# Layer 1 in slots of 12 matmuls, and the split of the next pair's operands at the end of `down`

## The chip, the cores and the metric

The kernel runs on one core of a Trainium2 chip. The metric is the device time of one execution in microseconds (us). The engines are TensorE (PE: matrix products; PEld are its weight loads), VectorE (DVE), ScalarE (ACT), GpSimd (POOL) and SyncE (SP), whose in-order queue issues all transfers between DRAM and the on-chip memory SBUF. Matrix products arrive in PSUM, a second on-chip memory.

## What is computed

Attention without a softmax, whose heads are normed by their root mean square, then a layer that takes the maximum of three projections, then a second normed layer with a gate. All data are 32-bit floats.

```python
kv = np.einsum('bhsd,bhse->bhde', k, v)            # 8 batches, 8 heads, 576 tokens, head size 64
out = np.einsum('bhsd,bhde->bhse', q, kv)
x = out / sqrt(mean(out * out, -1) + 1e-6) * g_norm   # laid out as 4608 tokens x 512
h = np.maximum(np.maximum(x @ w1, x @ w2), x @ w3)    # 512 -> 768
x = h @ w_out                                         # 768 -> 512
xn = x / sqrt(mean(x * x, -1) + 1e-6) * rms_g
g = xn @ w_gate                                       # 512 -> 1536
out = (g * sigmoid(g) * (xn @ w_val)) @ w_out2        # 1536 -> 512
```

## The kernel before

**Precision.** Every operand is held as a hi and a lo part; the product of two operands is three matmuls (hi hi, hi lo, lo hi; lines 300 to 302, and `prod3` at L611 in layer 2). To split a tile, ACT writes the hi and DVE or POOL subtracts it from the tile for the lo (`split_h`, L318 and L319, with the lo on POOL).

**Layer 1.** The 4608 tokens are nine blocks `t` of 512 (NB = 9). For a block, `do_p(t, j)` makes three projections of 12 matmuls (128x512 each) for each of six column groups j, in the PSUM tiles `p`. ACT copies the first (`s1`, L327), DVE takes the maximum with the second (`s2`, L331) and with the third (`h`, L335), and `split_h` makes `hs`. `do_o(t, j)` adds `hs` times `w_out` into four PSUM tiles `acc`, one group j later. After each projection `mid()` is called: it issues one piece of the other work.

That other work, for the block that comes next, is by token groups of 128: `ao_a` multiplies q with the head's kv (`po`, L252), takes its squares (ACT), sums them (L260), and POOL raises the mean to the power -0.5 (L264); `ao_b` scales (`xn`, L269); `do_tr` turns the result on PE (`pt`, L290) and splits it into the block's `x` (L292 on ACT, L293 on DVE). `load_q` and `load_kv` load q, k and v; `do_kv` multiplies k with v (`pk`, L233). Then there is `end1` (with `two`, `over`, `end1_rest`): at the end of a block, `acc` is copied and squared, summed over the tokens' values by PE with a matrix of ones (`pr`, L411), normed, split once more (`two`), spread by a second `pr`, and stored as `xn_d`. `pair_sums` makes the sums and differences of two stored blocks (`td`) for layer 2. Finally `store_pair`, 18 generators in the list `todo`, prepares the weights of layer 2: a raw load, a conversion of two 32-bit words to one float on ACT and DVE (L99 to L109), sums of quarters (L148 to L151), splits of the four quarters (`ws`, L159 and L160) and four stores (`wd`, L163). `pump()` steps the generators that are under way (up to `most[0]` = 2) and `pair_sums` (by `aside`); `flush()` steps the norm of `end1`.

The order of all this is that of the calls as they are written; each engine works its instructions off in this order, and waits at the first whose input isn't ready.

**Layer 2.** Block 0 is computed as it stands. The other eight blocks are taken in four pairs by a scheme of seven products in place of eight: `run_unit` makes seven products of prepared token operands (`xo`, in `XO[m, k]`) and weights (`w`, `wq`) in the PSUM tiles `ua`, `ub`, `uc`; the seventh one of a unit (`last_product`) is issued in the next. The hidden values get their own sums and differences (`t`, L486), and are split for the second product (`ho`, by `split_h`). Each part's split is put off by some `tick`s (`defer`). `down` multiplies these parts with the prepared `w_out2` (`wd`): three times for each pair, in the PSUM tiles `da`, `db` and `dc`, for two halves d of the rows: product 1 in `da` and 5 in `db` (`one`), 2 in `dc`, 6 in `da`, 3 in `db`, 7 and 4 in `da`. After each product, `slot()` ticks. `build_x` makes the operands of the next pair: three of the seven (m = 1, 2, 3) are split on the chip from the stored tokens (`xr`), hi on ACT (L545) and lo on POOL (L546), the other four are loads of `td`. It is a generator (`xs`) that is stepped in the last unit before the third `down` of a pair, and at every second slot of that `down`.

Of the kernel before, what the change touches and what calls it, by code (L numbers as in the profile page):

```python
# [34 lines left out]
def tile_kernel(ctx: ExitStack, tc, qT, k, v, gcol, w1, w2, w3, wo, wg, wv, wo2, rmsg, out):  # L35
# [67 lines left out]
    def conv_b(raw, tt):  # L103
        t, u = tt[:, 0], tt[:, 1].bitcast(I32)
        ti = t.bitcast(I32)
        nc.scalar.activation(t, t, AF.Copy, scale=2.0**-112)
# [18 lines left out]
    def store_pair(i, jp):  # L125
        if i < 2:
            srcs = [cols((wg, wv)[i], 2 * jp + k) for k in range(2)]
        else:
            srcs = [wo2[(2 * jp + k) * P:(2 * jp + k + 1) * P, :] for k in range(2)]
        raws = [load_raw(srcs[0])]  # L130
        yield
        yield
        tts = []
        for k in range(2):
            tts.append(conv_a(raws[k]))
            yield
            conv_b(raws[k], tts[k])
            if k == 0:
                raws.append(load_raw(srcs[1]))
                yield  # L140
            yield
        (t0, c0), (t1, c1) = ([tt[:, n].rearrange("p (o f) -> p o f", o=2) for n in range(2)] for tt in tts)
        if i < 2:
            quarters = [(t0[:, 0], t0[:, 1]), (t1[:, 0], t1[:, 1])]
        else:
            quarters = [(t0[:, 0], t1[:, 0]), (t0[:, 1], t1[:, 1])]
        (a11, a12), (a21, a22) = quarters
        nc.vector.tensor_tensor(c0[:, 0], a21, a22, ALU.add)  # L148
        nc.vector.tensor_tensor(c0[:, 1], c0[:, 0], a11, ALU.subtract)
        nc.vector.tensor_tensor(c1[:, 0], a11, a21, ALU.subtract)  # L150
        nc.vector.tensor_tensor(c1[:, 1], a12, c0[:, 1], ALU.subtract)  # L151
        yield
        for n, src in enumerate((quarters[0], c0, c1, quarters[1])):
            g = unit([P, 2, 2, 256], F32R, "ws")
            for o, (dst, sv) in enumerate([(g, src)] if n in (1, 2) or i < 2 else [(g[:, k], src[k]) for k in range(2)]):
                if isinstance(sv, tuple):
                    sv = (t0, t1)[n // 2]
                hi, lo = (dst[:, 0], dst[:, 1]) if len(dst.shape) == 3 else (dst[:, :, 0], dst[:, :, 1])
                nc.scalar.activation(hi, sv, AF.Copy)  # L159
                nc.vector.tensor_tensor(lo, sv, f32(hi), ALU.subtract)  # L160
            yield
            d = w_d[i, jp, n] = dp.tile([P, 2, 2, 256], F32, name="wd", tag=f"wd{i}_{jp}_{n}")
            nc.sync.dma_start(d, f32(g))  # L163
# [12 lines left out]
    def pump(n=1):  # L176
        for _ in range(n):
            aside()
            aside()
# [103 lines left out]

    def new_x(t):
# [37 lines left out]
    def do_p(t, j, mid, p=None):  # L322
# [13 lines left out]
        HT[t, j] = split_h(h, "hs")  # L336

# [54 lines left out]
    def end1(t):  # L392
        y, q = [], []
        for c in range(KC):
            y.append(yp.tile([P, TB], F32, tag="y", name="y"))
            nc.scalar.activation(y[c], acc[c], AF.Copy)
            q.append(yp.tile([P, TB], F32, tag="y", name="q"))
            nc.scalar.activation(q[c], acc[c], AF.Square)
            if c:
                nc.vector.tensor_tensor(q[0], q[0], q[c], ALU.add)  # L400
        norm.append(end1_rest(t, y, q[0], two(q[0])))

    def two(t):
        w = unit([P, 2, TB], F32R, "two")
        nc.scalar.activation(w[:, 0], t, AF.Copy)
        nc.vector.tensor_tensor(w[:, 1], t, f32(w[:, 0]), ALU.subtract)
        return w
# [7 lines left out]
    def end1_rest(t, y, q, w):  # L415
# [3 lines left out]
        q3 = q.rearrange("p (s n) -> p s n", s=NS)  # L419
# [8 lines left out]
        nc.gpsimd.tensor_tensor(rs, ms, mhalf.to_broadcast([P, NS]), ALU.pow)  # L428
        nc.vector.tensor_tensor(q3, bc(rs), id3, ALU.mult)
        w = two(q)  # L430
        yield
        pr = over(w)
        for c in range(KC):
            nc.vector.scalar_tensor_tensor(y[c], y[c], gb[:, c:c + 1], pr, ALU.mult, ALU.mult)
        yield
# [26 lines left out]
    def split_x2(i):  # L462
        t = X2.pop(i)
        x = X[NB + i // KC]
        nc.scalar.activation(x[:, 0, i % KC], t, AF.Copy)
        nc.vector.tensor_tensor(x[:, 1, i % KC], t, f32(x[:, 0, i % KC]), ALU.subtract)
# [22 lines left out]
    def pair_sums(t, y):  # L489
# [3 lines left out]
        def put(m, k, src):  # L493
            hi = tmp("th").bitcast(F32R)
            nc.scalar.activation(hi, src, AF.Copy)
            nc.vector.tensor_tensor(src.bitcast(F32R), src, f32(hi), ALU.subtract)
            return m, k, hi, src

        def store(m, k, hi, lo):
            d = t_d[n, m, k] = dp.tile([P, 2, TB], F32, name="td", tag=f"td{n}_{m}_{k}")  # L500
            nc.sync.dma_start(d[:, 0], f32(hi))
            nc.sync.dma_start(d[:, 1], lo)

        for k in range(2):
            b12, b22 = y[k], y[2 + k]
            b11, b21 = tmp("b11"), tmp("b21")
# [576 lines left out]
```

## Time and profile before

| | |
|---|---|
| median of 3 runs | 1544.07 us (1542.82 to 1544.5) |
| the profiled execution | 1542.86 us, span 1541.1 us |
| mean granted clock of PE | 0.985 of full |
| PE busy | 1486.0 us, 96% of the span |
| DVE, ACT, POOL busy | 938.5, 576.3, 460.9 us |
| moved by DMA | 313.79 MB, mean 204 GB/s |

The profile is one execution, with the start and end of every instruction. A wait is put down to the operation that ended it. The program's stages follow each other in time: first loads and first tokens until about 80 us, layer 1 with fewer tokens ready until 130 us, the rest of layer 1 until 690 us, block 0 of layer 2 until 830 us, then four pairs of some 175 us.

### The profile page before, as it was taken

To read this page: it belongs to the slowest core of one execution; us is meant where nothing else is said; L and a number is where in the kernel's file an instruction comes from. 1 tells how busy PE (TensorE), PEld (TensorE's weight loads), DVE (VectorE), ACT (ScalarE), POOL (GpSimd) and SP (SyncE) were. 2 spreads that over 40 slices of the span, in tenths; PEclk is the share of its full clock that TensorE was granted. 3 is DMA by queue.
4 is the path that set the end of the run, shared out by engine and by line. 5 is a ranking of instruction groups with operands and counts; after the bars stand their busy time and mean duration, and the time that the engine had idled before them with its cause. 6 is when DMAs were issued, how large, how long until landed. Compare 5 with 4: busy or idle time off the path is not lost.

```text
span 1541.1 us, 19959 instructions
## 1 busy us (share of the span) xinstructions
PE 1486.0 (96%) x7200; PEld 1226.3 (80%) x7200; DVE 938.5 (61%) x1418; ACT 576.3 (37%) x1027; POOL 460.9 (30%) x360
## 2 busy tenths in 40 slices
PE   5899999998999989999999999999999999999998
PEld 5787888786787878878888888788887888778887
DVE  4875556676657675773333656754756746755756
ACT  3443333434344434341322432433433432434432
POOL 2444222221312121211231422523425323433323
PEclk8999999999999999999999999999999999999999
DMA  9322247258445733564686854586546845576442
GB/s 318 119 69 93 73 158 254 95 207 305 171 143 206 264 124 116 215 244 191 241 316 219 316 199 177 219 315 244 195 186 251 322 186 211 219 281 238 166 176 102
DMA packets 132513, 313.79 MB, mean 204 GB/s; under 512 B 12352, under 2 KB 43072, under 8 KB 132416
## 3 DMA queue, kind: packets, MB, share of 16 engines
q1 hardware_dynamic: 132416, 312.53, 56.1%
q8 instruction: 57, 0.93, 0.2%
q14 instruction: 40, 0.33, 0.1%
HBM read 239.08 MB, written 73.40 MB: 203 GB/s over the span
## 4 chain that ended last, share of the span: by engine, by line
PE 50%; POOL 3%; issue 2%; ACT 1%; DVE 0%; POOLq 0%; DVEq 0%
PE ua L611 15%; PE ub L611 8%; PE da L611 8%; PE uc L611 4%; PE db L611 4%; POOL ho L319 2%; PE dc L611 2%; PE acc L301 1%; PE acc L300 1%; PE acc L302 1%; PE pv L302 1%; PE p L302 1%; PE pg L302 1%; PE pv L300 1%; PE pg L300 1%
## 5 line engine op out<-in xcount | busy, mean ns | idle before, releaser
L300 PE MATMUL p<-x,w 128*128 128x512 f32 (+1 forms) x652 | 263.1, 404 | 14.5 <-DVE h L335 9.8
L301 PE MATMUL p<-x,w 128*128 128x512 f32 (+1 forms) x652 | 258.4, 396 | 0.3 <-DVE x L293 0.3
L302 PE MATMUL p<-x,w 128*128 128x512 f32 (+1 forms) x652 | 258.3, 396 | 0.0
L611 PE MATMUL ua<-xo,w 128*128 128x512 f32 x864 | 213.4, 389 | 0.0
L319 POOL TENSOR_TENSOR ho<-sl,ho 128x512 fp32r<-128x512 f32 x72 | 99.2, 1385 | 319.9 <-issue 185.1
L611 PEld LDWEIGHTS ua<-xo,w 128*128 128x128 f32 x864 | 162.2, 188 | 33.6
L319 POOL TENSOR_TENSOR hs<-h,hs 128x512 fp32r<-128x512 f32 x54 | 69.6, 1288 | 394.9 <-ACT hs L318 371.8
L319 POOL TENSOR_TENSOR ho<-t,ho 128x512 fp32r<-128x512 f32 x96 | 125.5, 1311 | 117.9 <-ACT ho L318 110.6
L300 PEld LDWEIGHTS p<-x,w 128*128 128x128 f32 x652 | 126.4, 194 | 42.8 <-DVE h L335 11.3
L302 PEld LDWEIGHTS p<-x,w 128*128 128x128 f32 x652 | 126.0, 193 | 26.6
L301 PEld LDWEIGHTS p<-x,w 128*128 128x128 f32 x652 | 126.4, 194 | 25.9 <-DVE x L293 1.0
L611 PE MATMUL ub<-xo,w 128*128 128x512 f32 x576 | 146.1, 389 | 0.0
L611 PEld LDWEIGHTS ub<-xo,w 128*128 128x128 f32 x576 | 108.1, 188 | 22.4
L693 ACT ACTIVATE s<-ua 128x512 f32<-128x512 f32 x96 | 57.2, 596 | 151.4 <-PE ua L611 136.8
L318 ACT ACTIVATE hs<-h 128x512 fp32r<-128x512 f32 x54 | 34.1, 632 | 195.7 <-DVE h L335 183.3
L611 PE MATMUL da<-ho,wd 128*128 128x512 f32 x432 | 105.8, 389 | 0.0
L318 ACT ACTIVATE ho<-t 128x512 fp32r<-128x512 f32 x96 | 59.3, 627 | 103.3 <-DVE t L486 100.6
L611 PEld LDWEIGHTS da<-ho,wd 128*128 128x128 f32 x432 | 81.1, 188 | 16.9
L264 POOL TENSOR_TENSOR rs<-ms,mhalf 128x8 f32<-128x8 f32 x36 | 61.7, 1720 | 107.8 <-DVE ms L262 102.1
L300 PE MATMUL acc<-hs,w 128*128 128x512 f32 x216 | 84.9, 393 | 0.0
L641 DVE TENSOR_TENSOR c<-uc,s 128x512 f32<-128x512 f32 x48 | 33.1, 689 | 84.7 <-PE uc L611 84.7
L301 PE MATMUL acc<-hs,w 128*128 128x512 f32 x216 | 84.2, 390 | 0.5 <-POOL hs L319 0.5
(135 smaller groups left out, 2689.0 us busy)
## 6 DMA issues: line engine op xcount, KB each, us to landing
w<-wd SPq DMA_DIRECT2D x180, 512.0 KB, 7.7
wd<-ws SPq DMA_DIRECT2D x72, 512.0 KB, 3.7
wd<-wd SPq DMA_DIRECT2D x72, 512.0 KB, 6.9
wq<-wd SPq DMA_DIRECT2D x72, 256.0 KB, 7.9
xo<-td SPq DMA_DIRECT2D x32, 512.0 KB, 7.3
raw<-in_w SPq DMA_DIRECT2D x18, 512.0 KB, 8.2
q<-in_qT SPq DMA_DIRECT2D x18, 512.0 KB, 6.0
raw<-in_wo SPq DMA_DIRECT2D x18, 512.0 KB, 6.3
```

Source lines behind the costliest of these rows:

```text
L264: nc.gpsimd.tensor_tensor(rs, ms, mhalf.to_broadcast([P, H]), ALU.pow)
L300: nc.tensor.matmul(o, ah, bh, start=first, stop=False)
L301: nc.tensor.matmul(o, ah, bl, start=False, stop=False)
L302: nc.tensor.matmul(o, al, bh, start=False, stop=last)
L318: nc.scalar.activation(hs[:, 0], h, AF.Copy)
L319: nc.gpsimd.tensor_tensor(hs[:, 1], h, f32(hs[:, 0]), ALU.subtract)
L611: nc.tensor.matmul(o, aa, bb, start=first and q == 0, stop=last and q == 2, skip_group_check=True)
L641: nc.vector.tensor_tensor(t, p, s, ALU.add)
L693: nc.scalar.activation(t, p, AF.Copy)
```

## The change

**Layer 1.** A slot is 12 matmuls. `do_p` calls `mid` after each of its projections (a new argument `last` is called after the third), and `slot()` is called once more after `do_o`: four slots for each j, 24 for a block. `slot()` calls `tick`, `flush`, `aside` and `prep`. `tick` now also fires a table, `plan`: `at(n, fn)` sets `fn` for the n-th slot from now. A group of 128 tokens is five steps in five slots (`token`): products, scales, `ao_b`, turned, low. q is loaded at slots 0 and 5 of a block, its readers are the tokens at slots 1, 5, 9 and 13; k and v are loaded four slots ahead of `do_kv`. `end1` becomes a generator of ten steps, one a slot, where `flush` was called some slots apart. `pair_sums` has one step a slot, with its tiles in the pools `raw` and `y`. `store_pair` becomes the class `Prep` with 14 steps, of which at most two are live, and which can start only while there is room for its buffers; in it, the lo of each odd quarter is made on POOL and no longer on DVE, and a store comes a slot after its lo.

**Layer 2.** In block 0 the same `slot` is called. In `down` the two groups of product 6 come before the two of product 2. `build_x` issues its loads first, and then the three splits, each lo a step after its hi; it is not stepped in `run_unit` any more, but in `down` from slot 3 on, without slots 7, 9 and 11.

```diff
+            for g in range(2):
+                self.steps.append((0, lambda g=g: (self.put(i, jp, g), self.lo(g + 1), self.hi(g + 2))))
...
+        def lo(self, n):
+            for hi, lo, src in self.halves(n):
+                (nc.gpsimd if n % 2 else nc.vector).tensor_tensor(lo, src, f32(hi), ALU.subtract)
...
+    def token(n, i):
+
+        for m, fn in enumerate(token_steps(i)):
+            at(n + m, fn)
...
-    def do_p(t, j, mid, p=None):
+    def do_p(t, j, mid, p=None, last=None):
...
         HT[t, j] = split_h(h, "hs")
+        if last is not None:
+            last()
...
-        for m, r in ((1, 0), (5, None), (2, 1), (6, None), (3, 2), (7, None), (4, None)):
+        for m in (5, 6, 7, 4):
             for k in range(2):
-                x = unit([P, 2, TB], F32R, "xo")
-                if r is None:
-                    nc.sync.dma_start(f32(x), t_d[n, m, k])
-                else:
-                    nc.scalar.activation(x[:, 0], raw[:, r, k], AF.Copy)
-                    nc.gpsimd.tensor_tensor(x[:, 1], raw[:, r, k], f32(x[:, 0]), ALU.subtract)
-                XO[m, k] = x
+                x = XO[m, k] = unit([P, 2, TB], F32R, "xo")
+                nc.sync.dma_start(f32(x), t_d[n, m, k])
             yield
+        for m, r in ((1, 0), (2, 1), (3, 2)):
+            for k in range(2):
+                x = XO[m, k] = unit([P, 2, TB], F32R, "xo")
+                nc.scalar.activation(x[:, 0], raw[:, r, k], AF.Copy)
+            yield
+            for k in range(2):
+                x = XO[m, k]
+                nc.gpsimd.tensor_tensor(x[:, 1], raw[:, r, k], f32(x[:, 0]), ALU.subtract)
...
+        for fn in plan.pop(n_slot[0], ()):
+            fn()
+        n_slot[0] += 1
+
+    def at(n, fn):
+        plan.setdefault(n_slot[0] + n, []).append(fn)
+
+    def slot():
+        tick()
+        flush()
+        aside()
+        prep()
...
-            if xs is not None and n_x[0] % 2 == 0:
+            if xs is not None and n_x[0] > 2 and n_x[0] not in (7, 9, 11):
                 next(xs, 0)
...
         one(1)
         for d in range(2):
+            prod_down(d, ph, 6, acc[d][0])
+            keep(d, 1, acc[d][0])
+            slot()
+        for d in range(2):
             c = psum([P, TB], "dc")
             prod_down(d, ph, 2, c, True)
             put(d, 0, c)
             slot()
-        for d in range(2):
-            prod_down(d, ph, 6, acc[d][0])
-            keep(d, 1, acc[d][0])
-            slot()
...
+                at(0, lambda i=base // 2: load_q(i))
+                at(5, lambda i=base // 2 + 1: load_q(i))
+                at(3, lambda t=t: new_x(t + 1))
+                for n in range(NS):
+                    token(4 * n + 1, base + n)
...
-                do_p(t, j, pump)
-                if 1 <= j <= 4:
-                    flush()
+                do_p(t, j, slot, None, slot)
```

How the instructions stand on the engines, at three places. A row is a line of the program, an operation, the tile that it writes and those that it reads, and the size; x12 is a run of twelve.

PE in the third `down` of the first pair, before:

```order
L611 MATMUL da<-ho,wd 128x512 x6
L611 MATMUL db<-ho,wd 128x512 x6
L611 MATMUL dc<-ho,wd 128x512 x12
L611 MATMUL da<-ho,wd 128x512 x12
L611 MATMUL db<-ho,wd 128x512 x12
```

The same place in the changed kernel:

```order
L760 MATMUL da<-ho,wd 128x512 x6
L760 MATMUL db<-ho,wd 128x512 x6
L760 MATMUL da<-ho,wd 128x512 x12
L760 MATMUL dc<-ho,wd 128x512 x12
L760 MATMUL db<-ho,wd 128x512 x12
```

The twelve matmuls of product 6 in `da` now stand ahead of those in `dc`. POOL at the same place, before:

```order
L546 TENSOR_TENSOR xo<-xr,xo 128x512 x2
L319 TENSOR_TENSOR ho<-t_8383,ho 128x512
L319 TENSOR_TENSOR ho<-sl,ho 128x512
L319 TENSOR_TENSOR ho<-t_8490,ho 128x512
L319 TENSOR_TENSOR ho<-t_8514,ho 128x512
L546 TENSOR_TENSOR xo<-xr,xo 128x512 x2
L319 TENSOR_TENSOR ho<-sl,ho 128x512 x2
L319 TENSOR_TENSOR ho<-t_8516,ho 128x512
L546 TENSOR_TENSOR xo<-xr,xo 128x512 x2
```

And in the changed kernel:

```order
L421 TENSOR_TENSOR ho<-sl,ho 128x512
L421 TENSOR_TENSOR ho<-t_8464,ho 128x512
L421 TENSOR_TENSOR ho<-t_8488,ho 128x512
L421 TENSOR_TENSOR ho<-sl,ho 128x512 x2
L421 TENSOR_TENSOR ho<-t_8490,ho 128x512
L421 TENSOR_TENSOR ho<-t_8522,ho 128x512
L683 TENSOR_TENSOR xo<-xr,xo 128x512 x6
```

The six `xo` stood in three pairs between the hidden parts, and stand behind them all in one row. DVE in layer 1, in the j of block 4 that follows its first, before (L107 to L109 and L99 are the weight conversion):

```order
L107 TENSOR_SCALAR wt<-wt 128x512
L108 SCALAR_TENSOR_TENSOR wt<-raw,wt 128x512
L109 ISA wt<-wt 128x1024
L99 TENSOR_SCALAR wt<-raw 128x512
L331 TENSOR_TENSOR s_3311<-p_3298,s_3287 128x512
L107 TENSOR_SCALAR wt<-wt 128x512
L108 SCALAR_TENSOR_TENSOR wt<-raw,wt 128x512
L109 ISA wt<-wt 128x1024
L335 TENSOR_TENSOR h<-p_3319,s_3311 128x512
```

In the changed kernel:

```order
L110 TENSOR_SCALAR wt<-wt 128x512
L111 SCALAR_TENSOR_TENSOR wt<-raw,wt 128x512
L112 ISA wt<-wt 128x1024
L433 TENSOR_TENSOR s_3292<-p_3279,s_3241 128x512
L374 SCALAR_TENSOR_TENSOR x<-pt,gc,x 128x4x128
L513 TENSOR_TENSOR q<-q 128x512 x2
L181 TENSOR_TENSOR wt<-wt 128x256
L182 TENSOR_TENSOR wt<-wt 128x256
L183 TENSOR_TENSOR wt<-wt 128x256
L184 TENSOR_TENSOR wt<-wt 128x256
L437 TENSOR_TENSOR h<-p_3316,s_3292 128x512
```

The conversions still stand ahead of `s`; between `s` and `h` there are now the sums of squares of `end1` (L513), the lo of a token group (L374) and the sums of quarters (L181 to L184). SP's queue where a q is loaded, in the sixth block of layer 1, before:

```order
L217 DMA q<-in_qT 128x4x256
L163 DMA wd<-ws 128x1024 x7
L90 DMA raw<-in_wv 128x4x256
L163 DMA wd<-ws 128x1024
L90 DMA raw<-in_wo 128x1024
L217 DMA q<-in_qT 128x4x256
```

In the changed kernel:

```order
L628 DMA td<-th 128x512
L629 DMA td<-y 128x512
L635 DMA b<-xn_87 128x512 x2
L203 DMA wd<-ws 128x1024 x2
L268 DMA q<-in_qT 128x4x256
L203 DMA wd<-ws 128x1024
L628 DMA td<-th 128x512
```

The load of q stands right behind two stores of `ws` and the loads of `pair_sums`.

## Rows read from the trace of the kernel before

**Rows 1.** The page: span, and busy us, share of the span and instructions.

```profile
span 1541.1 us, 19959 instructions
...
PE 1486.0 (96%) x7200; PEld 1226.3 (80%) x7200; DVE 938.5 (61%) x1418; ACT 576.3 (37%) x1027; POOL 460.9 (30%) x360
```

**Rows 2.** Windows: stretch, length, busy PE, PEld, DVE, ACT, POOL, granted clock, DMA.

```profile
80.00:130.00 50.00, 46.22 (x193) 37.59 (x192) 35.68 (x46) 22.56 (x41) 23.10 (x20) 0.93 0.18 53
130.00:690.00 560.00, 542.10 (x2922) 448.16 (x2921) 365.94 (x644) 223.07 (x408) 127.76 (x101) 0.98 0.52 183
690.00:830.00 140.00, 140.00 (x618) 115.82 (x617) 50.59 (x71) 34.39 (x59) 30.53 (x24) 1.00 0.64 241
830.00:1541.00 711.00, 697.59 (x3062) 573.54 (x3061) 433.95 (x575) 263.72 (x464) 249.89 (x187) 1.00 0.60 222
```

**Rows 3.** Waits of PE: what it waited for, total us, times, longest us.

```profile
PE p L300 <- DVE h L335: 9.8, 7, 2.0
...
PE dc L611 <- POOL ho L319: 5.5, 8, 1.1
PE po L252 <- DVE s L331: 3.9, 2, 2.0
PE db L611 <- POOL ho L319: 3.8, 3, 1.3
...
PE pr L411 <- ACT s L327: 1.6, 1, 1.6
```

**Rows 4.** Timeline at the first pair's third down: start, us, instruction, idle before.

```profile
985.05 2.99 POOL L546 TENSOR_TENSOR xo<-xr,xo 128x512 fp32r<-128x512 f32 x2 [1.74 <-ACT xo L545]
...
989.26 1.74 POOL L319 TENSOR_TENSOR ho<-sl,ho 128x512 fp32r<-128x512 f32 x1
989.88 1.67 DVE L486 TENSOR_TENSOR t<-sl 128x512 f32<-128x512 f32 x1
...
994.05 0.74 PE L611 MATMUL db<-ho,wd 128*128 128x512 f32 x2 [1.27 <-POOL ho L319]
```

**Rows 5.** The same timeline, further on, at `dc`.

```profile
998.76 1.07 PE L611 MATMUL dc<-ho,wd 128*128 128x512 f32 x4
...
1000.84 2.11 PE L611 MATMUL dc<-ho,wd 128*128 128x512 f32 x8 [1.01 <-POOL ho L319]
```

**Rows 6.** Timeline of PE in layer 1, block 4.

```profile
380.94 1.16 PE L252 MATMUL po<-kvbd,q 128*128 128x128 f32 x8 [1.93 <-DVE s L331]
383.52 0.79 PE L300 MATMUL p<-x,w 128*128 128x512 f32 x1 [1.42 <-DVE h L335]
...
388.80 0.55 PE L300 MATMUL p<-x,w 128*128 128x512 f32 x1
```

**Rows 7.** Windows in layer 1; the granted clock is the number before the last two.

```profile
120.00:160.00 40.00, 36.22 (x155) 29.21 (x155) 20.61 (x27) 12.61 (x23) 14.54 (x12) 0.91 0.32 99
280.00:320.00 40.00, 37.95 (x175) 31.32 (x174) 28.37 (x52) 18.01 (x34) 10.63 (x8) 0.96 0.51 183
383.00:388.00 5.00, 4.48 (x11) 3.51 (x12) 3.26 (x5) 1.08 (x2) 2.29 (x2) 0.50 0.00 0
```

**Rows 8.** Groups from 130 to 690 us: line, operation, count, busy us, mean ns.

```profile
L319 POOL TENSOR_TENSOR hs<-h,hs 128x512 fp32r<-128x512 f32 x43 | 55.4, 1288 | 334.6 <-ACT hs L318 311.5 <-issue 16.4 <-DMA td<-t 6.6
...
L160 DVE TENSOR_TENSOR ws<-wt,ws 128x512 fp32r<-128x512 f32 x60 | 40.1, 686 | 8.5 <-ACT ws L159 8.5
...
L252 PE MATMUL po<-kvbd,q 128*128 128x128 f32 x200 | 27.3, 280 | 3.9 <-DVE s L331 3.9
...
L233 PE MATMUL pk<-v,k 128*64 128x64 f32 x384 | 12.5, 224 | 0.0
...
L496 DVE TENSOR_TENSOR b<-b,th 128x512 fp32r<-128x512 f32 x12 | 10.3, 858 | 7.2 <-ACT th L495 6.9
L160 DVE TENSOR_TENSOR ws<-wt,ws 128x256 fp32r<-128x256 f32 x24 | 9.1, 421 | 0.1
```

**Rows 9.** Line 217, the loads of q: issue to landing.

```profile
DMA to landing us min/median/max: 3.5/6.0/9.3
```

More of the change, by code (lines that the diff above doesn't have):

```diff
@@ L165, in start, with prep @@
+    preps = []
+    wait = []
+    def prep():
+        for p in list(preps):
+            p.step()
+            if p.n == len(p.steps):
+                preps.remove(p)
+        if wait and (not preps or len(preps) < 2 and preps[-1].n >= 8) and live[0] + 2 <= room[0]:
+            preps.append(wait.pop(0))
+            preps[-1].step()
     def start(g):
@@ L392, in end1 @@
     def end1(t):
[L393 to L407, printed above, removed]
+        norm.append(end1_steps(t, list(acc)))
     def over(w):
@@ L413, in over, with end1_steps, small, plus @@
         return pr
-    def end1_rest(t, y, q, w):
+    def end1_steps(t, acc):
         def bc(r):
             return r.rearrange("p (s o) -> p s o", o=1).to_broadcast([P, NS, P])
-        q3 = q.rearrange("p (s n) -> p s n", s=NS)
+        def small(name):
+            return yp.tile([P, TB], F32, tag="y", name=name)
+        def plus(c):
+            nc.vector.tensor_tensor(q[0], q[0], q[c], ALU.add)
+        def hi():
+            w = unit([P, 2, TB], F32R, "two")
+            nc.scalar.activation(w[:, 0], q[0], AF.Copy)
+            return w
+        def lo(w):
+            nc.vector.tensor_tensor(w[:, 1], q[0], f32(w[:, 0]), ALU.subtract)
+        y, q = [], []
+        for c in range(KC):
+            y.append(small("y"))
+            nc.scalar.activation(y[c], acc[c], AF.Copy)
+            q.append(small("q"))
+            nc.scalar.activation(q[c], acc[c], AF.Square)
+            if c == 2:
+                plus(1)
+            if c % 2:
+                yield
+        plus(2)
+        plus(3)
+        w = hi()
+        yield
+        lo(w)
+        yield
+        q3 = q[0].rearrange("p (s n) -> p s n", s=NS)
         id3 = ident.rearrange("p (o n) -> p o n", o=1).to_broadcast([P, NS, P])
@@ L597, in tile_kernel @@
     later = []
+    plan = {}
+    n_slot = [0]
     def defer(fn, n=2):
@@ L716, in run_unit @@
         tick()
-        if xs is not None:
-            next(xs)
         c = psum([P, TB], "uc")
@@ L727, in run_unit @@
         tick()
-        if xs is not None:
-            next(xs)
         prod(u, 3, b)
@@ L921, in tile_kernel, with pumped, kv_load, kv_do @@
         do_p(1, 0, pump)
-        for j in range(2, J1):
-            do_p(0, j, pump)
+        def pumped():
+            tick()
+            flush()
+            pump()
+        def kv_load(b):
+            at(0, lambda: load_kv(b))
+        def kv_do(n, b):
+            at(n, lambda: do_kv(b, kvb[b % 2]))
+        for j in range(2, J1):
+            if j == J1 - 1:
+                kv_do(0, 2)
+                for m in range(NS):
+                    token(1 + 2 * m, 2 * NS + m)
+                at(2, lambda: load_q(5))
+                at(3, lambda: new_x(2))
+            do_p(0, j, pumped)
@@ L939, in tile_kernel @@
+        do_p(1, J1 - 1, pumped, None, pumped)
+        while flight or todo:
+            pump()
+        wait += [Prep(i, jp) for jp in range(J2 // 2) for i in range(3)]
         for j in range(J1 - 1):
             do_o(1, 1, j, J1)
[L941 to L952 removed]
@@ L953, in tile_kernel @@
-        most[0] = 2
-        for jp in range(J2 // 2):
-            todo += [store_pair(i, jp) for i in range(3)]
+            slot()
         for t in range(2, NB):
             last = t + 1 == NB
+            if not last:
+                base = NS * (t + 1)
+                b = (NS * P * (t + 2) - 1) // S
+                m = -(-(b * S - P + 1) // P) - base
+                if m >= 0:
+                    at(max(0, 4 * m - 5), lambda: room.__setitem__(0, 4))
+                    at(max(0, 4 * m - 4), lambda b=b: load_kv(b))
+                    at(4 * m, lambda b=b: (do_kv(b, kvb[b % 2]), room.__setitem__(0, 8)))
+                at(0, lambda i=base // 2: load_q(i))
[3 more added lines that the diff above has]
+                    token(4 * n + 1, base + n)
+            else:
+                at(3, lambda: new_x(NB))
+                for c in range(KC):
+                    at(4 * c, lambda c=c: load_x2(c))
+                    at(4 * c + 4, lambda c=c: hi_x2(c))
+                    at(4 * c + 5, lambda c=c: lo_x2(c))
@@ L1021, in tile_kernel @@
                     do_o(2, NB, j - 1, J2)
+                slot()
             if j == 2:
```

277 lines of the change are left out of this document (152 added, 125 removed).

## Prediction

> **What bounds the kernel now.** TensorE (PE) does: it is busy for 1486.0 us of a span of 1541.1 us [rows 1], so that every gain must come out of the 55 us in which it stands, and out of stretches in which its clock is low. I read three views in this order. The busy time by stretch [rows 2] says where PE stands: 3.8 us in 80 to 130 us, 17.9 us in the rest of layer 1 (130 to 690 us), nothing in block 0 of layer 2, and 13.4 us in the four pairs of blocks. (Before 80 us the two kernels issue the same work.) The fully busy stretch, 140.0 us for 618 matmuls, gives the price of a 128x512 matmul: 0.227 us, and 2.72 us for 12.
>
> The waits of PE [rows 3] say for what. In the pairs there are two kinds only: `dc` for the lo half of a hidden part (8 times, 5.5 us) and `db` for the same (3 times, 3.8 us). In layer 1 PE waits for results of VectorE (DVE): `p` for `h` (7 times, 9.8 us), `po` for `s` (3.9 us) and smaller ones; nothing there is a lack of DVE as a whole, which is busy for 366 of 560 us [rows 2].
>
> The timelines say why. In a pair [rows 4] GpSimd (POOL) spends 2.99 us on two lo halves of the next pair's operands (`xo`) from 985.05; the hidden parts come late behind them, one runs from 989.26 to 991.00, the DVE difference `t` that starts at 989.88 cannot end before 991.55, its own lo on POOL comes after that, and `db` stands until 994.05. At `dc` [rows 5] another pair of `xo` sits in front of the lo that `dc` needs: four matmuls from 998.76 would have run until 999.67, the fifth starts at 1000.84. In layer 1 [rows 6] two weight conversions on DVE (the `order` rows of DVE ahead) stand before `s` and `h`: `po` waits 1.93 us, `p` 1.42 us, and then 12 matmuls take from 383.52 to 388.80, 5.28 us instead of 2.72. The granted clock is 0.50 there [rows 7], its lower level (1.2 of 2.4 GHz), so one such dip costs 2.6 us on top of the stall. Three windows of 40 us (from 120, 360, 520) have a mean granted clock of 0.91 and two (from 280, 440) of 0.96; [rows 7] has the first of either kind. Together that is 3 x 3.6 + 2 x 1.6 = 14 us of full speed; some 3 us of it is idle time counted already, which leaves 11. So 80 to 690 us costs 3.8 + 17.9 + 11 = 33 us above bare matmuls. No matmul is added or removed.
>
> **Product 6 before product 2, and the split of the next pair's operands last.** The two groups of product 6 (12 matmuls, 2.72 us) now lie between the last `db` and `dc`. The latest `dc` above is 1000.84 - 999.67 = 1.17 us late, the 2.72 us cover it twice over, and product 6 reads a part that POOL makes before that of product 2. The `xo` halves (six for each of the four pairs, 1.3 to 1.5 us each) leave the units and come at the end of `down`, six in a row, behind the hidden parts of that `down`. With them gone, the lo that ended at 991.00 ends some 2 us sooner, `t` and its own lo move up as much, and `db`, which stood for 1.27 us, finds it in time by some 0.7 us. Who is late next? The reader of the six is the following unit. The first two are issued at slot 10 of 15, five groups of 1.36 us (6.8 us) ahead of the unit's product 1, which needs them and for which POOL takes 2.6 us; products 2 and 3, with the other four, come 2.7 and 5.4 us later. If one is late all the same, it costs PE some 1 us in each of three pairs. The loads of the sums (`td`) are now issued before these, in the slots 3 to 6 of `down`, earlier than a unit needs them. Gain: the waits of 9.3 us plus about 0.16 us at each of 11 for the restart (1.17 us lost against 1.01 us idle in [rows 5]): 11.1 us, of a stage that has 13.4 us idle. Bounds 7 and 13; I take 11.
>
> **Layer 1 in slots.** What it removes is the queueing: an `s`, `h` or `xn` has 12 matmuls, 2.72 us, between its last input and its reader, and one small step of each job goes beside it. What it doesn't remove is DVE's work at a block's end, where the ten steps of `end1`, the tokens of the next block and up to two weight jobs meet. I count one such place from the order of the changed kernel, the first block end after weight jobs begin (t = 2): from the `s` of j = 1 to the lo of the second `two`, DVE has 20 full-width instructions and 7 half-width ones, at 0.69 and 0.42 us [rows 8] 13.8 + 2.9 = 16.7 us, two tiny ones not counted. Over the same way PE has 62 full matmuls, 14.1 us, 12 of `po` and `pt` at 27.3 / 200 = 0.14 us and 40 of `pk` at 12.5 / 384 = 0.03 us [rows 8]: 17.0 us. There is no reserve, so any hold-up of DVE there is a stall of PE.
>
> Such a hold-up is in the change. The lo of every odd quarter goes from DVE (0.69 us) to POOL (1.29 us, by the `hs` row of [rows 8]): 36 instructions, which takes 25 us from DVE and gives POOL 46 us on top of 128 of 560. But DVE subtractions of two SBUF tiles take longer beside a POOL subtraction: the `t` of [rows 4] took 1.67 us, ending 0.55 us after POOL did, and the 12 `b` lo's of layer 1 have a mean of 0.86 us where their like takes 0.69 [rows 8]. In the kernel before, no weight lo lies beside a POOL subtraction (686 ns over 60 of them); in the new one they, the bit operations of the second job and the sums of squares do. Price: 0.2 us (the `b` rows) to 1.0 us (the `t` row) each time. The Trainium skill, "SBUF — State Buffer" (Who interferes with whom), states that a DVE instruction with two SBUF inputs and a GpSimd instruction reading SBUF share a port pair under an exclusive lock, and that the loser blocks for the whole instruction. The trace agrees, with the 1.67 us; by that rule alone, every one of the 36 moved lo's could block DVE for up to its 1.29 us, and the move would cost DVE 46 us to save it 25.
>
> I put the rest of layer 1 together as follows. Block ends: 2 us of stall at each of the five with weight jobs, from 0.5 (the count above, handovers only) to 4 (several blocked instructions): 10. Clock: the dip of [rows 6] came with stalls of 1.93 and 1.42 us in a row, so I expect one only where a block end goes as badly as that: two instead of five, at 2.6: 5. Chains without reserve elsewhere (`xn` to the turn of a token behind POOL's power, `hs` behind a busy ACT): 3, between 0 and 8. The second `pr` at the start of layer 2: 1.5, as the smaller waits of [rows 3] go. Loads of `q`: they are now issued one slot before their reader on the one in-order queue, behind puts that wait for a lo of the slot before (`order` rows of SP). From issue to landing the trace has 3.5 / 6.0 / 9.3 us [rows 9], and the reader is three slots, 8.2 us, behind the step whose lo holds the queue; POOL's lo, the put and the issue can use up 4.6 of these, so 3.6 to 8.2 us are left (an estimate from [rows 8] and the slots): 3, from 0 to 40. Sum 22.5 us, so layer 1 gives 33 - 22.5 = 10.5 us, bounds -20 and +25. ACT and POOL get no path of their own here: ACT is busy for 223 of 560 us [rows 2].
>
> **The sum** against the profiled execution, 1542.86 us: - 11 - 10.5 = 1521.4. The median of the runs is 1544.07 us, 1.2 us more, so the forecast is 1522 us.
>
> **Rivals.**
> - *Only the pairs gain.* DVE's sum at block ends equals PE's, so with the blocked instructions it becomes the bound there, and the stalls come back at other readers at their old size, 33 us. For it: no reserve in the count, and the port. Against it: on the whole of layer 1 DVE has a third of its time free. 1544 - 11 = 1533 us, from 1529 to 1540.
> - *All of it gains.* The slots hold, `q` lands in time, the clock stays up: some 8 to 10 us remain in layer 1. 1544 - 11 - 24 = 1509 us. For it: the average DVE load. Against it: the count above.
> - *Slower: the loads of `q`.* Two per block in six blocks, 12 in all, stand behind puts in the queue. A load that lands after the median 6.0 us, with 3.6 us to go, stops PE for 2.4 us, and with a dip of 2.6 us behind it costs 5.0. The sum above has a gain of 21.5 us and 3 us of this already, so it decides from five late loads (24.5 / 5.0); with eight it is 40 - 24.5 = 15.5 us slower, 1560 us. For it: the median against the worst place. Against it: not every load finds the queue held, and in the trace no wait of `po` is for `q` [rows 3].
> - *The change doesn't do it.* The `dc` and `db` waits turn into waits for other parts and layer 1 keeps its stalls: 1543 us.
>
> **Chances.** The forecast (1514 to 1529) 0.45; only the pairs 0.25; all of it 0.15; slower 0.09; no effect 0.06. A difference of 0.2% (3 us) is about what a measurement of this kernel can tell from none. Faster by more than that holds the first three and little else: 0.85; within it 0.06; slower 0.09. The range, with all but 2 in 10, is 1508 to 1537 us.
>
> **What would show it.** After: no `dc` or `db` wait for POOL in the list of waits, and 830 us to the end some 11 us shorter; the `xo` lo's in one row at the end of `down`. In layer 1, fewer `p` and `po` waits for `h` and `s`, fewer windows under 1.00 of granted clock; the rest of the stalls at `pr` and `pt` at block ends, with DVE instructions of 1.0 us and more beside POOL's lo. Wrong would be: waits of `po` for the DMA of `q` (the slower rival), block ends that stand as long as before (only the pairs), or a wait of `ua` for `xo`.

## The result, and the profile after

The changed kernel takes 1518.66 us (1517.52 to 1519.37), the kernel before beside it 1543.44 us: a ratio of 0.9839, with a 95% interval from 0.9822 to 0.9856. That is 24.8 us faster; 1522 us was forecast, the range was 1508 to 1537. The next fence is from the page of the changed kernel: span, and busy us, share and count by engine; it answers to [rows 1].

```profile
span 1516.9 us, 20013 instructions
...
PE 1475.2 (97%) x7200; PEld 1218.5 (80%) x7200; DVE 942.8 (62%) x1376; ACT 575.3 (38%) x1027; POOL 522.3 (34%) x402
```

PE's busy time falls too, by 11 us, with the same 7200 matmuls; a matmul counts for longer where the clock is low. The windows of the changed kernel (columns as in [rows 2]) show where the rest went.

```profile
80.00:130.00 50.00, 46.21 (x194) 37.64 (x193) 36.29 (x46) 21.96 (x40) 22.49 (x20) 0.94 0.24 72
130.00:690.00 560.00, 547.20 (x2979) 449.92 (x2978) 383.57 (x614) 226.24 (x415) 196.00 (x145) 1.00 0.53 182
...
830.00:1516.00 686.00, 683.03 (x3014) 565.43 (x3012) 424.60 (x568) 259.35 (x457) 243.32 (x186) 1.00 0.61 227
```

Against [rows 2], PE stands 3.0 us in the pairs and no longer 13.4, and 12.8 us between 130 and 690 us instead of 17.9. In that stretch the mean granted clock is 1.00, and it is 1.00 in 280 to 320 us too, where [rows 7] has 0.96: of the dips after 130 us none is left. From 80 to 130 us next to nothing changed. Windows of fixed times cut the stages at other places, so the ends of the stages are better taken from the last `acc` matmul of layer 1 and of block 0, first before, then after. They also correct the 690 and 830 us that stand ahead of the prediction for the ends of layer 1 and of block 0: in the kernel before these lie at 736.6 and 838.4 us.

```profile
736.56 0.39 PE L302 MATMUL acc<-hs,w 128*128 128x512 f32 x1
...
838.39 0.39 PE L302 MATMUL acc<-gs,w 128*128 128x512 f32 x1
```

```profile
724.09 0.39 PE L404 MATMUL acc<-hs,w 128*128 128x512 f32 x1
...
827.20 0.39 PE L404 MATMUL acc<-gs,w 128*128 128x512 f32 x1
```

Layer 1 ends 12.5 us sooner, block 0 takes 1.3 us longer (103.1 us against 101.8), and from there to the end of the span it is 689.7 us against 702.7: 13.0 us from the pairs. The waits of PE in the changed kernel, as in [rows 3] (us in total, times, longest):

```profile
PE pt L392 <- DVE xn L320: 9.4, 4, 3.4
...
PE pt L368 <- DVE xn L320: 6.9, 13, 0.9
PE p L402 <- DVE s L433: 3.8, 1, 3.8
PE pr L502 <- DVE two L521: 3.5, 5, 1.0
PE po L348 <- DVE wt L111: 2.0, 1, 2.0
PE pr L501 <- DVE s L433: 1.4, 2, 0.9
```

No `dc`, no `db`, no `p` that waits for `h`. The first and the 3.8 us of `p` belong to the time before 130 us. What is new is `pt` for `xn`: 13 waits, none over 0.9 us. The stalls of layer 1 are not much less in sum, they are many short ones in place of a few of 2 us, and the clock stays up.

### The profile page after: what moved, and what is told of

Same layout as the page of the kernel before. It is cut to its first block, busy times and chain, and to the rows that moved or that the text cites. A ratio compares the mean times of both kernels' runs of the same rounds, so it can differ in the third digit from the quotient of the medians.

```text
span 1516.9 us, 20013 instructions
## 1 busy us (share of the span) xinstructions
PE 1475.2 (97%) x7200; PEld 1218.5 (80%) x7200; DVE 942.8 (62%) x1376; ACT 575.3 (38%) x1027; POOL 522.3 (34%) x402
## 4 chain that ended last, share of the span: by engine, by line
PE 63%; DVE 3%; issue 2%; POOL 1%; DMA 1%; ACT 1%; POOLq 0%; DVEq 0%; SPq 0%
PE ua L760 17%; PE da L760 9%; PE ub L760 9%; PE uc L760 4%; PE db L760 4%; PE p L402 3%; PE p L404 3%; PE p L403 3%; PE dc L760 2%; PE acc L403 2%; PE acc L402 2%; PE acc L404 2%; POOL rs L362 1%; PE pv L404 1%; PE pg L402 1%
## 5 line engine op out<-in xcount | busy, mean ns | idle before, releaser
L421 POOL TENSOR_TENSOR hs<-h,hs 128x512 fp32r<-128x512 f32 x54 | 78.0, 1444 | 364.6 <-ACT hs L420 326.9
L402 PEld LDWEIGHTS p<-x,w 128*128 128x128 f32 x652 | 124.5, 191 | 28.7 <-DVE s L433 4.4
L404 PEld LDWEIGHTS p<-x,w 128*128 128x128 f32 x652 | 124.2, 190 | 26.3
L403 PEld LDWEIGHTS p<-x,w 128*128 128x128 f32 x652 | 124.5, 191 | 24.6 <-DVE x L395 1.0
L433 DVE TENSOR_TENSOR s<-p,s 128x512 f32<-128x512 f32 x54 | 37.2, 689 | 88.9 <-PE p L404 76.2
```

The lines of the kernel that those rows point to most:

```text
L402: nc.tensor.matmul(o, ah, bh, start=first, stop=False)
L403: nc.tensor.matmul(o, ah, bl, start=False, stop=False)
L404: nc.tensor.matmul(o, al, bh, start=False, stop=last)
L421: nc.gpsimd.tensor_tensor(hs[:, 1], h, f32(hs[:, 0]), ALU.subtract)
L433: nc.vector.tensor_tensor(s2, p, s1, ALU.max)
```

## The experiments

The changed kernel was run a second time, unaltered, beside the second group of kernels.

> The changed kernel once more, unaltered, beside the kernels that follow: ratio to the kernel before within 0.982 to 0.986, no granted clock of 0.5 between 130 us and the end of layer 1.

It took 1517.09 us, a ratio of 0.9826 (0.9809 to 0.9844). Its granted clock from 130 to 675 us is 1.00, as expected. Two measurements of one kernel thus differ by some 1.6 us, and ratios below are read against 0.9826 to 0.9839.

**The pairs, order of products alone undone** (`dc_old`).

```diff
         for d in range(2):
-            prod_down(d, ph, 6, acc[d][0])
-            keep(d, 1, acc[d][0])
-            slot()
-        for d in range(2):
             c = psum([P, TB], "dc")
             prod_down(d, ph, 2, c, True)
             put(d, 0, c)
+            slot()
+        for d in range(2):
+            prod_down(d, ph, 6, acc[d][0])
+            keep(d, 1, acc[d][0])
             slot()
```

> The changed kernel with the old order in down alone: product 2 before product 6. Theory (the order cures the dc waits, the moved xo splits only the part by which the third down of a pair is worse): the 8 dc waits come back at about 0.64 us of lost time each, with no xo in front of them, so 5 us: 1524 us, no db wait. Rival A (the order is all of it): also the 1.2 us of the three third downs, 6.8 us: 1525.5. Rival B (the xo splits were the cause of all, the order does nothing): 1519 and no dc wait.

Measured: 1522.82 us, 0.9869 (0.9855 to 0.9884), so some 5 us over the changed kernel. The waits of PE from 830 us on, and a `dc` of the run:

```profile
PE dc L760 <- POOL ho L421: 3.8, 8, 0.5
```

```profile
926.24 1.07 PE L760 MATMUL dc<-ho,wd 128*128 128x512 f32 x4
927.79 1.43 PE L760 MATMUL dc<-ho,wd 128*128 128x512 f32 x5 [0.48 <-POOL ho L421]
```

All eight waits are back, and none is over 0.5 us: the 1.0 us of the third `down` [rows 5] was half `xo`. The theory holds, rivals A and B fall. The rows also show what a wait costs on top of the time that PE stands. The four matmuls from 926.24 would have run until 927.15, so 0.64 us are lost for 0.48 us of idle time; and the five after it take 1.43 us, where five `dc` matmuls in the changed kernel take 1.30:

```profile
987.91 1.30 PE L760 MATMUL dc<-ho,wd 128*128 128x512 f32 x5
```

So this wait costs its idle time and 0.16 + 0.13 = 0.29 us. The sums below take that for every wait of PE, which is an estimate from this one.

**The pairs, the old `build_x` and its old steps** (`xo_old`).

```diff
-        for m in (5, 6, 7, 4):
+        for m, r in ((1, 0), (5, None), (2, 1), (6, None), (3, 2), (7, None), (4, None)):
...
+        if xs is not None:
+            next(xs)
...
-            if xs is not None and n_x[0] > 2 and n_x[0] not in (7, 9, 11):
+            if xs is not None and n_x[0] % 2 == 0:
```

> The changed kernel with the old build_x, stepped in the last unit and at every second slot, and the new order of products. Theory (xo lo's in POOL's queue delay the hidden parts): db waits come back, 3 times 1.4 us, no dc wait since 2.72 us of product 6 cover 1.2: 1523 us. Rival A (product 6 now reads a part behind the xo lo's and waits in place of dc): 3 to 4 us more, 1526. Rival B (db was cured by something else): 1519.

Measured: 1522.15 us, 0.9865 (0.9851 to 0.9880), again some 4 to 5 us over the changed kernel. Its waits from 830 us on:

```profile
PE db L757 <- POOL ho L421: 3.8, 3, 1.3
```

That is the `db` row of [rows 3], number for number, and no `dc`: 12 matmuls of product 6 do cover the `xo` lo's. The two edits of the pairs cure two waits, each its own.

**The pairs alone, on the kernel before** (`pairs_only`).

```diff
-                        run_unit(n, jp, i, xs)
+                        run_unit(n, jp, i)
...
+        for d in range(2):
+            prod_down(d, ph, 6, acc[d][0])
...
```

> The kernel before with the change of the pairs alone (order of products, build_x last). Theory (two independent gains, 12.7 us from the pairs by the traces): 1531 us, layer 1 as before. Rival (the gains depend on each other, since loads of the pairs follow layer 1): more than 3 us away from 1531.

Measured: 1529.54 us (1524.80 to 1531.81), 0.9907 (0.9887 to 0.9926): 14 us, as from 13.0 and the 1.6 us by which two measurements differ. In its trace the stretch from the end of block 0 (833.3 us) to the end of the span (1523.0 us) is 689.7 us, the same as in the changed kernel. So the gain of the pairs doesn't depend on layer 1. But the profiled execution took only 1524.80 us, and its layer 1, which is the code of the kernel before, ended 5 us sooner than in the trace of before:

```profile
731.47 0.39 PE L302 MATMUL acc<-hs,w 128*128 128x512 f32 x1
```

Its waits in layer 1 are nearly those of [rows 3] (`p` for `h` 10.2 us in 8, `po` for `s` 3.9 us in 2, the longest 2.0 us in both), and its windows (the first is 120 to 160 us, as in [rows 7]) say where the 5 us come from:

```profile
120.00:160.00 40.00, 36.68 (x228) 30.01 (x229) 21.01 (x29) 11.90 (x21) 14.55 (x13) 1.00 0.35 108
...
360.00:400.00 40.00, 33.80 (x151) 27.06 (x152) 28.67 (x51) 18.18 (x34) 9.71 (x9) 0.91 0.42 144
...
520.00:560.00 40.00, 35.90 (x159) 29.09 (x158) 28.85 (x53) 18.45 (x35) 9.41 (x9) 0.91 0.45 155
```

Only the two windows with 0.91 are under 1.00, in place of five (those from 280 and 440, left out here, are 1.00 too), after stalls of nearly the same lengths. Whether a single stall of 2 us, or one of 3.8, brings the clock down differs from one execution to the next.

**Layer 1, every lo of the prepared weights on DVE** (`lo_dve`).

```diff
-                (nc.gpsimd if n % 2 else nc.vector).tensor_tensor(lo, src, f32(hi), ALU.subtract)
+                nc.vector.tensor_tensor(lo, src, f32(hi), ALU.subtract)
```

> The changed kernel with every lo of the prepared weights on DVE, none on POOL. Theory (the shared port takes back what the move gives): the DVE time of 130 us to the end of layer 1 is not above the 384 us of the changed kernel although 25 us of subtractions come back to it, since fewer DVE instructions are held up beside POOL's lo's; PE's stalls change by less than 2 us: 1517 to 1521. Rival (the move to POOL relieves DVE where it is the bound): DVE some 25 us above 384, stalls at pr, po and pt up by 4 to 8 us: 1523 to 1527.

Measured: 1516.00 us, 0.9822 (0.9805 to 0.9838): the same as the changed kernel, as the theory had it; PE stands for 12.4 us in the window below and for 12.8 in the changed kernel. The window of layer 1 in this run, and two of its groups on DVE (columns as in [rows 8]):

```profile
130.00:690.00 560.00, 547.62 (x2977) 449.51 (x2976) 391.53 (x655) 227.05 (x415) 146.84 (x103) 1.00 0.52 182
```

```profile
L199 DVE TENSOR_TENSOR ws<-wt,ws 128x512 fp32r<-128x512 f32 x60 | 49.2, 829 | 1.9 <-ACT ws L195 1.9
...
L99 DVE TENSOR_SCALAR wt<-raw 128x512 f32<-128x512 f32 x19 | 7.9, 418 | 0.0
```

The same groups in the changed kernel; the first answers to the L160 row of [rows 8]:

```profile
L199 DVE TENSOR_TENSOR ws<-wt,ws 128x512 fp32r<-128x512 f32 x30 | 27.2, 908 | 3.5 <-ACT ws L195 3.5
...
L99 DVE TENSOR_SCALAR wt<-raw 128x512 f32<-128x512 f32 x19 | 14.5, 761 | 0.0
```

DVE is busy for 391.5 us against 383.6 in the changed kernel, so some 25 us of subtractions back on it cost 8, and POOL loses 49 us. That is more than the "not above 384" that was expected, and far from 409. A lo on DVE took 0.69 us in the kernel before, takes 0.83 here and 0.91 in the changed kernel; the first step comes with the new order: in this run's trace every lo of 1.1 us and more lies beside POOL's `hs` or POOL's share of the clip (L99), where one that lies beside neither takes 0.69 at most. The second step, and a clip of L99 of 0.76 us instead of 0.42, come with POOL's lo's: of the longer ones in the changed kernel most lie beside these, the others beside `hs` or POOL's clip. So most of what the move took from DVE comes back to it. The Trainium skill, "SBUF — State Buffer" (Who interferes with whom), has the rule for this, an exclusive lock on a port pair, and the direction agrees. The worst case that the prediction worked out (46 us more on DVE) did not come: the net relief was 8 us, and the time shows none of it.

**Layer 1, the reader right behind the result** (`no_gap`, then `xn_soon`). Both put the scales of a token group and `xn`, which reads POOL's power, into one slot. The first moves the turn (`pt`) a slot forward as well (and, for the first block, its `new_x`), the second leaves it.

```diff
-        for m, fn in enumerate(token_steps(i)):
+        for m, fn in zip((0, 1, 1, 2, 3), token_steps(i)):
```

> The changed kernel with the scales of a token group and their reader (xn) in one slot and the two later steps a slot sooner: DVE gets the reader right behind the operation whose result POOL still works on. Theory (a slot between result and reader is what layer 1 gained from): DVE stands some 1.8 us at each of the 28 token groups, the s or h behind it comes late, p and po wait again: 5 to 15 us, 1524 to 1534. Rival (DVE has a third of its time free, so a standing DVE costs nothing, and the 6.9 us of pt waiting for xn go because xn is issued sooner): 1512 to 1519.

```diff
-        for m, fn in enumerate(token_steps(i)):
+        for m, fn in zip((0, 1, 1, 3, 4), token_steps(i)):
```

> The changed kernel with xn in the slot of the scales, and the turn of the token group where it is in the changed kernel: against no_gap, this leaves pt its distance and takes only DVE's. Theory A (what no_gap lost is the distance of pt alone, 25 waits of 2.6 us and the clock after each): DVE stands some 1.8 us behind POOL's power at each of the 28 groups, and nobody is late for it: 1512 to 1520. Theory B (a standing DVE makes s and h late, as the prediction has it): p and po wait again, 1524 or more.

Measured: `no_gap` 1604.90 us, 1.0397 (1.0380 to 1.0413); `xn_soon` 1553.88 us, 1.0068 (1.0053 to 1.0084). One slot in the wrong place costs 87 and 36 us; both make the change slower than the kernel before, far outside what was expected of `no_gap` (1524 to 1534). Waits of PE in layer 1, `no_gap` first, with one of its `pt` from the timeline:

```profile
PE pt L368 <- DVE xn L320: 65.3, 25, 4.5
```

```profile
210.11 1.09 PE L368 MATMUL pt<-ident,xn 128*128 128x128 f32 x4 [2.59 <-DVE xn L320]
...
211.42 0.63 PE L403 MATMUL p<-x,w 128*128 128x512 f32 x1
211.84 0.63 PE L404 MATMUL p<-x,w 128*128 128x512 f32 x1
```

And `xn_soon`, with the DVE instructions ahead of one of its waits:

```profile
PE pr L502 <- DVE two L521: 28.1, 8, 5.8
```

```profile
307.03 0.69 DVE L320 TENSOR_TENSOR xn<-po,rs 128x512 f32<-128x512 f32 x1 [4.91 <-POOL rs L362]
307.64 0.68 DVE L521 TENSOR_TENSOR two<-q,two 128x512 fp32r<-128x512 f32 x1
...
308.38 0.66 PE L502 MATMUL pr<-two,ones 128*128 128x512 f32 x1 [4.82 <-DVE two L521]
```

In `no_gap`, PE itself stands at the turn, 2.6 us a time, and the matmuls behind it go at 0.42 us, the lower clock (a granted clock of 0.50 from 210.8 to 212.7 us). In `xn_soon` `pt` has its slot, and DVE stands: 4.9 us in front of `xn`, with the lo of `two` queued behind it, and PE waits for that lo. Theory B was right that a standing DVE costs, although DVE has a third of its time free; it was wrong on who waits, which is `pr` and not `p` or `po`.

**Layer 1, the same work in clumps** (`clump`).

```diff
-        prep()
+        if n_slot[0] % 2:
+            prep()
+            prep()
```

> The changed kernel with the weight jobs stepped twice in every second slot: the same DVE work, in clumps of two steps. Theory (the evenness of the slots is the gain): two steps of 1.9 us in front of an s or h that has 2.7 us, so p and po wait 0.5 to 1.5 us at some ten of 18 jobs' steps: 1522 to 1530, with the clock down in places. Rival (only the slot between result and reader counts, not the evenness): 1517 to 1520.

Measured: 1537.93 us, 0.9966 (0.9954 to 0.9978): 20 us over the changed kernel, where 5 to 13 was expected. Its waits in layer 1:

```profile
PE pt L368 <- DVE xn L320: 8.1, 8, 2.3
PE pr L502 <- DVE two L521: 7.8, 6, 2.7
PE po L348 <- DMA q<-in_qT: 6.0, 2, 5.4
```

With the weight jobs in clumps PE waits up to 2.7 us at block ends and up to 5.4 us for a load of q, and from 130 to 675 us the granted clock is 0.98 and no longer 1.00. So this clumping costs more than all that layer 1 gained (12.5 us). The run doesn't part what the clumps do on DVE from what they do to the queue of loads. The waits are at `pr`, `pt` and `po`, though, not at `p` for `h`.

**Layer 1, later readers** (`both_late`).

```diff
-        for m, fn in enumerate(token_steps(i)):
+        for m, fn in zip((0, 1, 2, 4, 5), token_steps(i)):
...
         lo(w)
         yield
+        yield
```

The second edit stands at both `lo(w)` of `end1_steps`.

> The changed kernel with one slot more ahead of the turn of a token group (pt) and ahead of both pr of end1. Theory (these readers are a slot too close: from the end of p2 the chain h, sum, power on POOL behind hs, xn has 5.4 us and takes 5.5 to 6.3): the waits pt for xn (6.9 us, 13 times) and pr for two and s (4.9 us) go, with 0.27 us of restart each: 12 to 16 us less idle, 1503 to 1508. Rival (the chain is full: what is taken from pt shows up at the next reader, po or p): 1514 to 1519.

Measured: 1513.15 us, 0.9808 (0.9790 to 0.9825), 4 us under its neighbour `after_same`; the intervals overlap. Waits in layer 1:

```profile
PE p L402 <- DVE s L433: 5.0, 3, 3.3
PE po L348 <- DMA q<-in_qT: 4.7, 2, 3.0
```

The waits of `pr` are gone and those of `pt` are down to 0.2 us, as the theory had it, and others take their place, as the rival had it. The time lies between the ranges of the two.

**Layer 1, POOL's power ahead of `hs`** (`hs_last`). In the changed kernel, `do_p` splits `h` before the slot that follows, so that POOL's queue has `hs` ahead of the power of a token group. A timeline of the changed kernel:

```profile
236.93 1.30 POOL L421 TENSOR_TENSOR hs<-h,hs 128x512 fp32r<-128x512 f32 x1 [7.67 <-ACT hs L420]
...
238.19 1.63 POOL L362 TENSOR_TENSOR rs<-ms,mhalf 128x8 f32<-128x8 f32 x1
...
239.85 0.69 DVE L320 TENSOR_TENSOR xn<-po,rs 128x512 f32<-128x512 f32 x1 [1.62 <-POOL rs L362]
...
240.60 0.66 PE L368 MATMUL pt<-ident,xn 128*128 128x128 f32 x4 [0.53 <-DVE xn L320]
```

```diff
-        HT[t, j] = split_h(h, "hs")
         if last is not None:
             last()
+        HT[t, j] = split_h(h, "hs")
```

> The changed kernel with the split of h behind the steps of the slot that follows it, so that POOL takes the power of a token group ahead of the 1.3 us of hs, which has a reader only one j later. Theory (pt waits for xn since the power stands behind hs): the 13 waits of pt (7.0 us) fall under 2 us: 5 to 8 us faster than the changed kernel, 1509 to 1513. Rival (DVE's queue is what holds xn): the pt waits stay above 4 us, 1515 to 1519.

Measured: 1506.11 us (1504.31 to 1507.39), 0.9760 (0.9745 to 0.9774): some 11 us faster than the changed kernel (5 to 8 was expected), and the fastest of all. The waits of layer 1, and the same place:

```profile
PE pr L502 <- DVE two L521: 2.1, 3, 0.9
PE pt L368 <- DVE xn L320: 1.2, 2, 0.9
```

```profile
237.08 1.63 POOL L362 TENSOR_TENSOR rs<-ms,mhalf 128x8 f32<-128x8 f32 x1 [7.74 <-DVE ms L360]
238.68 1.30 POOL L421 TENSOR_TENSOR hs<-h,hs 128x512 fp32r<-128x512 f32 x1
238.75 0.69 DVE L320 TENSOR_TENSOR xn<-po,rs 128x512 f32<-128x512 f32 x1 [0.44 <-POOL rs L362]
```

The power starts 1.1 us sooner and `pt` doesn't wait; `hs` has its reader only in the next j. Two kinds of wait that weren't aimed at went as well, `po` for q and the `pr` for `s`; why is not shown.

**Everything together** (`best1`: `hs_last`, the two later `pr`, all lo's on DVE, and the loads of q three slots sooner; `hs_two`: `hs_last` and the two later `pr`).

```diff
-                at(0, lambda i=base // 2: load_q(i))
-                at(5, lambda i=base // 2 + 1: load_q(i))
+                if t == 2:
+                    at(0, lambda i=base // 2: load_q(i))
+                at(2, lambda i=base // 2 + 1: load_q(i))
+                if t + 2 < NB:
+                    at(20, lambda i=base // 2 + 2: load_q(i))
```

> All that pointed to a gain: hs behind the slot's steps, one slot more ahead of both pr, every lo of the prepared weights on DVE, and the loads of q 3 to 4 slots sooner. If the waits are separate: 17 us of idle in layer 1 fall to some 4 and the 1.2 us at the start of layer 2 goes, 1501 to 1506. Rival (the queue of DVE is full at the block ends, as in both_late, where s became late): 1508 to 1513.

> hs_last with one slot more ahead of both pr of end1, the odd lo's of the weights on POOL as in the changed kernel. Theory (what is left in hs_last, pr for two with 3.1 us and 1.2 us of lost time at the start of layer 2, is distance alone): 3 to 5 us under hs_last, 1501 to 1503. Rival (best1 lost to the step that was moved in end1, since its later steps then meet the tokens of other slots): s or pt late again, 1507 to 1512.

Measured: `best1` 1510.52 us, 0.9791 (0.9775 to 0.9807); `hs_two` 1515.79 us, 0.9829 (0.9812 to 0.9847). Both are slower than `hs_last`, as the rivals said, and `hs_two` is so by more than its rival had (1507 to 1512). The waits of `hs_two` in layer 1, and DVE and POOL ahead of the longest of `pt`:

```profile
PE pt L368 <- DVE xn L320: 6.7, 4, 2.9
PE p L402 <- DVE s L433: 2.9, 1, 2.9
```

```profile
359.11 1.78 DVE L626 TENSOR_TENSOR b<-b,th 128x512 fp32r<-128x512 f32 x1
...
360.30 1.71 POOL L199 TENSOR_TENSOR ws<-wt,ws 128x512 fp32r<-128x512 f32 x1
360.81 1.75 DVE L626 TENSOR_TENSOR y<-y,th 128x512 fp32r<-128x512 f32 x1
...
362.48 0.68 DVE L320 TENSOR_TENSOR xn<-po,rs 128x512 f32<-128x512 f32 x1
```

The later `pr` doesn't wait any more, but what follows `end1` falls into other slots: four lo's of `pair_sums` (L626) stand ahead of this `xn`, where `hs_last` has two. The power was done at 358.63 us. Two of the four take 1.78 and 1.75 us in place of 0.68, the first beside POOL's `hs` (1.82 us from 358.52), the second beside POOL's lo of a weight; `xn` starts at 362.48 and `pt` stands for 2.85 us. In `best1`, which has no weight lo on POOL, the same four stand there, only the one beside `hs` is long (1.77 us), and `pt` stands for 1.79 us. So a distance that is added at one place moves every step behind it, and POOL's lo's, which cost no time in the changed kernel (`lo_dve`), cost some 1.1 us at this place.

## Why the prediction was right, and where not

The forecast was 21.5 us by profiled executions (11 from the pairs, 10.5 from layer 1); the profiled spans differ by 1541.1 - 1516.9 = 24.2 us.

- *Pairs, 11 forecast, 13.0 measured.* The mechanism was the one described: each edit alone leaves the wait of the other (`dc_old`, `xo_old`), and `pairs_only` has the same 13 us from the pairs without the change of layer 1. The term for the restart was too small: not 0.16 us at each of 11 waits but 0.29, 3.2 us in place of 1.8. The fear that a unit then waits for `xo` was empty: no wait of `ua` is in the list.
- *80 to 130 us.* The sum counted this stretch in its 33 us of loss but gave it no term in the rest. It kept all of it: the wait of `p` for `s` of 3.8 us, and the lower clock after it (0.94 over the window). This is a step that failed, by some 6 us.
- *The clock, 5 us left of 11.* After 130 us nothing is left. The gain of layer 1 is mostly this: PE stands 5 us less between 130 and 690 us, and the rest of the 12.5 us is put down to the clock by difference. The long waits were cut into short ones, of 0.9 us at most but for one, and no dip followed. `pairs_only` shows that the number of dips also differs between executions of the same code, by 5 us there.
- *Block ends, 10 us left.* The six waits at `pr` in layer 1 sum to 3.9 us (4.9 less the one of 1.0 in block 0), with restarts some 5.6: at the place named, and less than priced. The hold-ups beside POOL's lo's are there (0.91 us for 0.69), but `lo_dve` shows that in the changed kernel they decide nothing. The count of the block end was wrong: in the trace, from the `s` at 215.24 us to the lo of the second `two` at 233.37, DVE has the 20 full-width instructions but three half-width ones, not seven; the four sums of quarters stand behind the lo. That is 15.1 us against PE's 17.0, a reserve of 1.9 us. Two instructions held up by some 1 us each (1.53 us for 0.42, 1.64 for 0.69) take it up, DVE stands for POOL's power as well (1.54 us), and PE waits 1.6 us in two at this end; at the other three ends with waits it is 0.4 to 1.2 us.
- *`xn` to `pt`, 3 us left, from 0 to 8.* 6.9 us in 13 waits, some 11 with restarts. The chain was named ("behind POOL's power"); what made it long was `hs` ahead of the power in POOL's queue, as `hs_last` shows by taking it away. This term failed too, by some 8 us.
- *The loads of q, 3 us left.* One load of the 12 was late. Only six have their reader one slot on, as the prediction has it for all: the load at slot 5 of a block has its first reader at slot 9, four slots on. The 2.0 us that the list puts down to `wt` (L111) at 510.10 us belong to it: SP's queue was held by two stores until the load was issued, 5 us ahead of its reader, inside the 3.5 to 9.3 us of [rows 9]:

```profile
498.68 6.32 SPq L203 DMA_DIRECT2D wd<-ws  x2
...
505.06 0.43 SPq L268 DMA_DIRECT2D q<-in_qT  x1
...
510.10 1.13 PE L348 MATMUL po<-kvbd,q 128*128 128x128 f32 x8 [1.97 <-DVE wt L111]
```

That the wait is for q is read from other runs: at the same place `dc_old` names q (1.63 us at 508.29), `lo_dve` too (1.69 us at 511.34); `both_late` has 3.0 and `clump` 5.4 us at such loads. So the slower rival is a real mechanism; it needed five late loads and had one.

- *The `pr` at the start of layer 2, 1.5 us.* 1.0 us and the restart; block 0 is 1.3 us longer.

So two terms were some 14 us too small together (80 to 130 us, `pt`), and three some 10 too large (clock, block ends, q): layer 1 and block 0 gave 12.5 - 1.3 = 11.2 us where 10.5 was forecast, a good sum of terms that are each less good, which is luck in part. By these terms layer 1 would have gained 4 us less than it did. The 33 us that they are taken from count idle time and clock but no restart; the 15 waits that the trace of before lists from 130 to 690 us would add 4.4 us at 0.29 each, an estimate that no run tries. Nor does a run part the edits of layer 1 from each other: `no_gap`, `xn_soon` and `clump` show what the distance and the evenness are worth in the new order, and not which edit brought the 12.5 us. "Only the pairs gain" falls, since `pairs_only` takes 1529.5 us and the changed kernel 11 us less. "All of it gains", 1509 us, took one edit more: `hs_last` reaches 1506.

## What to carry to other kernels

Give a result a slot of other work before its reader, but count the whole chain between two readers on PE, with what stands in front of each link in its engine's queue: here 1.3 us of a job without hurry (`hs`) in front of one with hurry (the power) cost 13 waits, 11 us in all. Spread the side work evenly, since a clump of the same work lost 20 us. A wait costs its idle time and a restart, and here many waits of under 1 us were cheaper than a few of 2 us, since no dip of the clock followed them.

## What was not expected of the hardware

A wait of PE cost 0.29 us beyond the idle time that the profile shows (`dc_old`, 0.16 us up to the first matmul behind it and 0.13 us behind that). Nearly the same waits of layer 1 (a 3.8 us wait that ends between 122 and 125 us among them) brought the granted clock from 2.4 to 1.2 GHz five times in one execution and twice in another, 5 us of difference in one stage, while a wait of 1.97 us in the changed kernel brought no dip at all. And of 25 us of subtractions moved from DVE to POOL, DVE got 17 back in longer instructions of its own (the clip of L99, 0.76 us for 0.42).
